# Five rows of a late load go through GpSimd's queue in two blocks of partitions, and two partitions through SyncE

## The chip, the cores and the metric

The kernel runs on one core of a Trainium2 chip. The core has a matrix engine (TensorE, PE in the profile), VectorE (DVE), ScalarE (ACT), GpSimd (POOL) and SyncE (SP), an on-chip memory of 128 partitions, and 16 DMA engines that move data between it and HBM. The metric is the device time of one execution in microseconds (us); smaller is better.

## The reference

The input is an image of 384 x 384 positions with 384 channels in bf16. Each channel's mean over all positions is multiplied by one weight and put through a sigmoid, and every position is multiplied by the 384 scales that result:

```python
H = W = C = 384
def reference(x, w1d):          # x: (1, H, W, C), w1d: (1,)
    g = jnp.einsum("bhwc->bc", x) / (H * W)
    gp = jnp.pad(g, ((0, 0), (0, 0)))
    s = gp[:, 0:C] * w1d[0]
    s = sigmoid(s)
    return x * s[:, None, None, :]
```

Nothing can be written before everything has been read once. The input has 113.2 MB, far more than the on-chip memory, so part of it has to be read a second time.

## The kernel before, in words

A partition gets 1152 of the 147,456 positions, and one position, 384 channels of one partition (768 bytes), is called a row here. One buffer, `arena`, has 275 rows in each partition.

**First pass.** Every row is loaded and summed: `sum_rows` (L253) issues one matmul per row with a matrix of ones, all into one accumulator (L242). 784 rows per partition are only streamed through; 368 rows stay on chip for the second pass. To make room, 296 of these are folded by `fold` (L292): the few exponent bits in which bf16 values of this size differ leave room in three rows for the content of a fourth. VectorE does that with bit operations (lines 276 and 282), ScalarE checks that the values fit (L313). The rows of a fourth are first loaded behind the group's other rows and become free when their group has been folded. For the last group of the second column they are the eight rows `V` (arena rows 212 to 219), so `V` can only be loaded again after the last fold's VectorE steps have read it.

**The end of the first pass** is a list of loads of plain kept rows, each followed by its matmuls, in this order (L443): eight rows at U, 20 at A, 11 at A + 20, eight at A + 31, eight at V, six at Y + 1, four at T + 5, three at T + 2, two at T, and then one last streamed row (L445). T and Y are scratch rows of `fold`. All are issued through SP's queue by `load` (L231, the DMA at L236), 128 partitions each. SP issues in order, and a DMA whose room isn't free yet holds up those behind it.

**The turn.** When the last matmul is done, ScalarE makes the scales `s_bf` (L451) and a copy in the accumulator's bank (L455). GpSimd then scales three blocks of four rows (U, U + 4 and V), and VectorE begins with all other kept rows (`scale`, L464).

**Second pass.** The 784 streamed rows are loaded again, scaled and stored, while the folded groups are unfolded, scaled and stored. The order of loads, stores and scalings is laid down at build time by a small simulation with fixed costs. It begins at the turn and doesn't depend on how the first pass was loaded.

**Order and waits.** The class `Flow` records each step with what it reads and writes (`add`, L34). `emit` (L68) then gives each engine its steps in the order of recording and puts in the semaphore waits. Each DMA is given one of 24 semaphores of its queue in turn, and it waits until the DMA that had this semaphore before has landed. Of a step's waits, the last is attached to its instruction and the others are wait instructions of their own (L112). For a step whose function returns no instruction, the last wait is dropped.

**GpSimd's queue before.** GpSimd issues no DMA in the first pass. Late in the second, the step `again` (L552, recorded at L738) waits for stores, reads a flag, and only if a value didn't fit when folded does it load, scale and store rows anew with GpSimd's own DMAs. For this input the branch isn't taken.

Of the kernel before, what the change touches and what calls it, by code (L numbers as in the profile page):

```python
# [9 lines left out]


class Step:
    __slots__ = ("eng", "emit", "dma", "lane", "deps", "wanted", "rank", "waits", "know", "i")

    def __init__(self, eng, emit, dma):
        self.eng, self.emit, self.dma = eng, emit, dma
        self.deps, self.wanted, self.rank, self.waits, self.know = [], False, 0, [], None
        self.lane = None


class Flow:
# [6 lines left out]
    def __init__(self, nc, tc):  # L28
# [2 lines left out]
        self.writer, self.readers = {}, {}  # L31
        self.queued = {}

    def add(self, eng, emit, reads=(), writes=(), dma=False, after=()):  # L34
        s = Step(eng, emit, dma)
        s.i = len(self.steps)
        deps = set(after)
        for c in reads:
            if c in self.writer:
                deps.add(self.writer[c])  # L40
        for c in writes:
            if c in self.writer:
                deps.add(self.writer[c])
            for r in self.readers.get(c, ()):
                deps.add(r)
        if dma:
            q = self.queued.setdefault(eng, [])
            s.lane = (eng, len(q) % self.LANES)
            s.rank = len(q) // self.LANES + 1
            if len(q) >= self.LANES:  # L50
                deps.add(q[-self.LANES])
            q.append(s)
        for d in deps:
            if d.eng == eng and not d.dma and not dma:

                if eng == "PE":
                    continue
            s.deps.append(d)
        for c in writes:
            self.writer[c] = s  # L60
            self.readers[c] = []
        for c in reads:
            if c not in writes:
                self.readers.setdefault(c, []).append(s)
        self.steps.append(s)
        return s

    def emit(self):  # L68
        nc = self.nc
        engines = {"SP": nc.sync, "ACT": nc.scalar, "PE": nc.tensor, "DVE": nc.vector, "POOL": nc.gpsimd}  # L70

        know = {e: {} for e in engines}

        def covers(k, d):
            return k.get(d.lane, 0) >= d.rank if d.dma else k.get(d.eng, -1) >= d.i

        for s in self.steps:
            k = know[s.eng]
            for d in sorted(s.deps, key=lambda d: -d.i):
                if covers(k, d):  # L80
                    continue
                s.waits.append(d)
                d.wanted = True
                for key, v in d.know.items():
                    if k.get(key, -1) < v:
                        k[key] = v
            s.know = dict(k)
            if s.dma:
                s.know[s.lane] = s.rank
            else:  # L90
                s.know[s.eng] = s.i

        count, sems = {}, {}
        for s in self.steps:
            if not s.dma and s.wanted:
                s.rank = count[s.eng] = count.get(s.eng, 0) + 1

        def sem(s):
            key = s.lane if s.dma else s.eng
            if key not in sems:  # L100
                name = f"f_{key[0]}{key[1]}" if s.dma else f"f_{key}"
                sems[key] = self.tc.alloc_semaphore(name)
            return sems[key]

        last = {}
        with self.tc.tile_critical():  # L106
            for s in self.steps:
                eng = engines[s.eng]
                waits = [(sem(d), d.rank * (16 if d.dma else 1)) for d in s.waits]
                hold = None if s.dma or not waits else waits.pop()  # L110
                for h, v in waits:
                    eng.wait_ge(h, v)  # L112
                ins = s.emit()
                if ins is None:
                    continue
                if hold:
                    ins = ins._wait_ge(*hold)
                if s.dma:
                    ins.then_inc(sem(s), 16)
                    last[s.lane] = s  # L120
                elif s.wanted:
                    ins.then_inc(sem(s), 1)
            for lane, s in sorted(last.items(), key=lambda at: at[1].i):
                engines[lane[0]].wait_ge(sem(s), 16 * s.rank)


# [1 line left out]
def kernel(  # L128
# [11 lines left out]
    nc = tc.nc  # L140
    P = nc.NUM_PARTITIONS
# [13 lines left out]
    PAIR = 2 * PIECE  # L155
    PAIRS = 4
    U = 3 * PIECE + PAIRS * 3 * PAIR
    G0 = U + PAIR
    V = G0 + PAIRS * 3 * PAIR
    A = V + PAIR  # L160
    N_A = 39
    T = A + N_A
    Y = T + 2 * PIECE
# [24 lines left out]
    arena = pool.tile([P, ROWS, C], bf16, name="arena")  # L188
    s_bf = pool.tile([P, C], bf16, name="s_bf")
    rest = pool.tile([P, P], bf16, name="rest")  # L190
    seen = pool.tile([P, 2 * len(pieces)], f32, name="seen")
    odd_i = pool.tile([P, 1], mybir.dt.int32, name="odd_i")
# [6 lines left out]
    xf = x.rearrange("b h w c -> (b h w) c")  # L199
    of = out.rearrange("b h w c -> (b h w) c")  # L200

    def view(t, r0, n):
        return t[r0 * P : (r0 + n) * P, :].rearrange("(p r) c -> p r c", r=n)

    def rows(lo, n):
        return [("a", r) for r in range(lo, lo + n)]

    fl = Flow(nc, tc)
# [5 lines left out]
    STREAMED, KEPT = (0, N_STREAM + 1), (N_STREAM + 1, N_KEPT - 1)  # L214
    LAST_ROW = ROWS - 1
    r = 0
# [7 lines left out]
    def raw(a):  # L224

        return c_raw + 1 + (a - U if a < G0 else PAIR + a - V)
# [4 lines left out]
    def load(chunk, a, lo, hi):  # L231

        r0, n = chunk
        fl.add(
            "SP",
            lambda: nc.sync.dma_start(out=arena[:, a : a + hi - lo, :], in_=view(xf, r0, n)[:, lo:hi, :]),  # L236
            writes=rows(a, hi - lo), dma=True,
        )
    def add_held(rhs, stop=False):

        pe = nc.tensor
        return pe.add_instruction(  # L242
            mybir.InstMatmult(
                name=nc.get_next_instruction_name(),
                ins=[pe.lower_ap(rhs), pe.lower_ap(ones[:])],
                outs=[pe.lower_ap(acc)],
                start_tensor_calc=False, stop_tensor_calc=stop,
                tile_size=(P, P), tile_position=(0, 0), ldweights=False,
            )
        )  # L250


    def sum_rows(a, n):  # L253
        def emit(i, first, last):
            if first:
                return nc.tensor.matmul(acc, lhsT=ones[:], rhs=arena[:, i, :], start=first, stop=last)  # L256
            return add_held(arena[:, i, :], last)

        for i in range(a, a + n):
            first, last = summed[0] == 0, summed[0] == RPP - 1  # L260
            fl.add(
                "PE", lambda i=i, f=first, l=last: emit(i, f, l),
                reads=[("a", i), "ones"], writes=["bank0"],
            )
            summed[0] += 1

    def keep_warm(n):


        for _ in range(n):  # L270
            fl.add("PE", lambda: add_held(s_bf[:]), reads=["s_bf", "ones"], writes=["bank0"])
# [20 lines left out]
    def fold(k):  # L292
# [46 lines left out]
        reads=["ones", "w_bf"], writes=["bank0"],  # L339
# [4 lines left out]
        reads=["bank0"], writes=["w_sc"],  # L344
# [6 lines left out]
    def stream(n, a):  # L351
        load(STREAMED, a, streamed[0], streamed[0] + n)
        if n > 40 and folding:
            keep_warm(N_WARM)
        sum_rows(a, n)
        streamed[0] += n
# [34 lines left out]
    for i, bk in enumerate(banks):  # L391
        lo, hi = i * BANK, min((i + 1) * BANK, PS * C)
# [7 lines left out]
    S1, S2 = [(A, 20)], [(A + 20, N_A - 20)]  # L400
# [38 lines left out]
    def take_raw(a, n):  # L439
        load(KEPT, a, raw(a), raw(a) + n)  # L440
        sum_rows(a, n)

    for a, n in [(U, 8)] + S1 + [(A + 20, 11), (A + 31, 8), (V, 8), (Y + 1, 6), (T + 5, 4), (T + 2, 3), (T, 2)]:  # L443
        take_raw(a, n)
    load(STREAMED, LAST_ROW, N_STREAM, N_STREAM + 1)  # L445
    sum_rows(LAST_ROW, 1)
# [5 lines left out]
        reads=["bank0", "w_sc"], writes=["s_bf"],  # L452
# [96 lines left out]
    N_OVER = 8  # L549
# [23 lines left out]
    written = []  # L573
# [128 lines left out]
    while True:  # L702

        if dve_at <= now:
# [4 lines left out]
            if landed and (ahead < PENDING or not can):  # L709
                chunk, a, lo, n, end = landed.popleft()  # L710
# [13 lines left out]
        if alongside and alongside[0][0] <= now:  # L724
            _, chunk, a, lo, n = alongside.popleft()
            store(chunk, a, lo, lo + n)
            moves.append([now + LAT, n * ROW + PER_STORE, stored(a, n)])
        while waiting and waiting[0][0] <= now:
            _, n, then, chunk, a, lo, known = waiting.popleft()
# [5 lines left out]
            asked = True  # L735
        if out_rows == total and not checked:
            checked = True
            fl.add("POOL", again, reads=["odd_i", "s_bf"], writes=rows(Y, N_OVER), after=written)  # L738
        while over and over[0][0] <= now:
            over.popleft()[1]()  # L740

# [1 line left out]
        if bank_at is None and len(line) <= total - BANKS_AT and got and max(got)[0] > PS * 4 // 3:  # L743
            a = max(got)[1]
# [3 lines left out]
            for i, bk in enumerate(banks):  # L748
                lo, hi = i * BANK, min((i + 1) * BANK, PS * C)
# [6 lines left out]
        if got and todo < N_STREAM:  # L756
            n, a = max(got)
            n = min(n, CAP, N_STREAM - todo)
# [56 lines left out]
```

## Time and profile before

| what | value |
|---|---|
| median of three runs | 720.7 us (720.28 to 720.85) |
| the profiled execution, its own time | 720.22 us |
| its span, first to last instruction | 718.4 us |
| last matmul of the first pass ends, from the span's start | 268.1 us |
| scales ready | 268.7 us |
| read from HBM, written to it | 190.32 MB, 113.25 MB |

The profile shows one execution. Busy time is given by engine; a group of instructions is named by its line, its engine and the buffers written and read. "Idle before" is the time in which the engine stood still before these instructions, with what ended it. The "DMA share" is the mean busy share of the 16 DMA engines and can go a little above 1, since packets overlap. The chain of waits is followed back from the last instruction to what released each step.

### The profile page before, as it was taken

The numbers are of one execution on the slowest core, as the hardware profiler recorded it, in microseconds if no ns is written. First come the engines' busy times: TensorE is split into PE (matmuls) and PEld (weight loads), VectorE is DVE, ScalarE is ACT, GpSimd is POOL, SyncE is SP. The second block draws the span as 40 slices with busy tenths as digits, with TensorE's granted clock in tenths as the row PEclk, the third lists the DMA queues.
The fourth block names the chain that finished last, engine by engine and source line by source line (L and its number), as shares of the span: only waits on it lengthen the run. The fifth ranks groups of instructions, "written<-read, shape, count | busy, mean of one in ns | idle before, by whom it ended". The sixth has DMA issues, their size and how long they took to land.

```text
span 718.4 us, 2070 instructions
## 1 busy us (share of the span) xinstructions
PE 214.4 (30%) x1202; PEld 0.3 (0%) x3; DVE 494.5 (69%) x474; ACT 116.5 (16%) x97; POOL 9.4 (1%) x7
## 2 busy tenths in 40 slices
PE   4667978989887880000000000000000000000000
PEld 0000000000000000000000000000000000000000
DVE  4600001978998929989998999989999965464430
ACT  3700001666777620001000000000000000000000
POOL 0000000000000004000000000000000000000000
PEclk9898999999999995555555555555555555555555
DMA  9999999999999989999999999999999999999997
GB/s 376 440 438 436 438 435 418 434 435 424 423 430 425 427 332 385 402 432 426 423 427 426 431 433 445 420 437 434 435 426 433 431 431 432 432 443 433 424 432 325
DMA packets 19741, 303.69 MB, mean 423 GB/s; under 512 B 2194, under 2 KB 3346, under 8 KB 6290
## 3 DMA queue, kind: packets, MB, share of 16 engines
q1 hardware_dynamic: 19728, 303.57, 99.1%
q8 instruction: 4, 0.07, 0.0%
q14 instruction: 7, 0.06, 0.0%
q10 hardware_dynamic: 2, 0.00, 0.0%
HBM read 190.32 MB, written 113.25 MB: 423 GB/s over the span
## 4 chain that ended last, share of the span: by engine, by line
DMA 72%; DVE 14%; PE 7%; ACT 2%; SPq 0%; issue 0%; another core or an unknown queue 0%; DVEq 0%
DMA arena<-in_x_dram 49%; DMA out_dram<-arena 23%; DVE arena L464 11%; PE bank L242 7%; ACT arena L313 2%; DVE arena L276 2%; DVE arena L282 1%; SPq L236 0%; SPq L474 0%; ACT s_bf L451 0%; SPq L112 0%; DVEq L112 0%; SPq L810 0%; SPq L106 0%
## 5 line engine op out<-in xcount | busy, mean ns | idle before, releaser
L464 DVE TENSOR_TENSOR arena<-arena,s_bf 128x4608 bf16<-128x4608 bf16 (+8 forms) x95 | 228.0, 2431 | 85.6 <-DMA arena<-in_x_dram 71.6
L242 PE MATMUL bank<-arena,ones 128*128 128x384 bf16 x1151 | 206.0, 343 | 44.9 <-DMA arena<-in_x_dram 44.8
L276 DVE TENSOR_SCALAR arena<-arena 128x1536 uint16<-128x1536 uint16 (+2 forms) x247 | 145.1, 632 | 105.5 <-DMA arena<-in_x_dram 99.5
L282 DVE TENSOR_TENSOR arena<-arena 128x1536 uint16<-128x1536 uint16 (+2 forms) x114 | 121.1, 1063 | 10.4 <-PE bank L242 7.6
L313 ACT ACTIVATE arena<-arena 128x3072 uint16<-128x3072 uint16 (+1 forms) x38 | 102.5, 2696 | 143.7 <-DVE arena L276 143.7
L541 PE MATMUL bank<-odd,ones 128*128 128x1 bf16 x1 | 0.2, 186 | 317.4 <-DVE odd L536 317.4
L388 ACT COPY arena<-bank 128x512 uint32<-128x512 uint32 (+2 forms) x8 | 4.2, 533 | 68.9 <-DMA out_dram<-arena 68.7
L464 POOL TENSOR_TENSOR arena<-arena,s_bf 128x1536 bf16<-128x1536 bf16 x3 | 9.2, 3099 | 268.7 <-ACT bank L455 268.7
L464 DVE TENSOR_TENSOR arena<-arena,bank 128x768 bf16<-128x768 bf16 (+5 forms) x12 | 12.5, 1113 | 0.0
L242 PE MATMUL bank<-s_bf,ones 128*128 128x384 bf16 x48 | 8.3, 326 | 0.0
L313 ACT ACTIVATION_READ_ACCUMULATOR arena<-arena 128x1 f32 x38 | 7.1, 186 | 0.0
L388 ACT COPY bank<-arena 128x512 uint32<-128x512 uint32 (+2 forms) x8 | 3.8, 529 | 0.0
L451 ACT ACTIVATE s_bf<-bank,w_sc 128x384 bf16<-128x384 f32 x1 | 0.6, 580 | 12.5 <-PE bank L242 12.5
L256 PE MATMUL bank<-arena,ones 128*128 128x384 bf16 x1 | 0.5, 480 | 6.9 <-DMA arena<-in_x_dram 6.9
L783 ACT ACT_TABLE_LOAD x1 | 1.3, 1283 | 0.7 <-PEq L799 0.7
L333 DVE MEMSET ones<- 128x128 bf16 x1 | 0.2, 165 | 1.1 <-SPq L106 1.1
L338 PE MATMUL bank<-w_bf,ones 1*128 1x1 bf16 x1 | 0.2, 182 | 2.1 <-DMA w_bf<-in_w1d_dram 2.1
L343 DVE TENSOR_SCALAR w_sc<-bank 128x1 f32<-128x1 f32 x1 | 0.2, 159 | 0.9 <-PE bank L338 0.9
L545 DVE CAST odd_i<-bank 128x1 int32<-128x1 f32 x1 | 0.2, 157 | 0.3 <-PE bank L541 0.3
L541 PEld LDWEIGHTS bank<-odd,ones 128*128 128x128 bf16 x1 | 0.1, 104 | 576.3 <-DVE odd L536 576.3
L455 ACT COPY bank<-s_bf 128x192 uint32<-128x192 uint32 x1 | 0.3, 323 | 0.0
L388 ACT COPY arena<-rest 128x64 uint32<-128x64 uint32 x1 | 0.2, 244 | 0.0
(10 smaller groups left out, 1.4 us busy)
## 6 DMA issues: line engine op xcount, KB each, us to landing
arena<-in_x_dram SPq DMA_DIRECT2D x6, 6144.0 KB, 33.8
arena<-in_x_dram SPq DMA_DIRECT2D x6, 4608.0 KB, 28.7
out_dram<-arena SPq DMA_DIRECT2D x8, 3072.0 KB, 30.8
arena<-in_x_dram SPq DMA_DIRECT2D x7, 3072.0 KB, 29.3
out_dram<-arena SPq DMA_DIRECT2D x3, 4608.0 KB, 43.4
arena<-in_x_dram SPq DMA_DIRECT2D x3, 4512.0 KB, 28.8
out_dram<-arena SPq DMA_DIRECT2D x3, 4512.0 KB, 35.4
out_dram<-arena SPq DMA_DIRECT2D x10, 1248.0 KB, 11.1
```

What stands on the lines that cost most here:

```text
L242: return pe.add_instruction(mybir.InstMatmult(name=nc.get_next_instruction_name(), ins=[pe.lower_ap(rhs), pe.lower_ap(ones[:])], outs=[pe. ...
L256: return nc.tensor.matmul(acc, lhsT=ones[:], rhs=arena[:, i, :], start=first, stop=last)
L276: lambda: nc.vector.tensor_scalar(out=dst, in0=src, scalar1=s0, scalar2=s1, op0=op0, op1=op1),
L282: "DVE", lambda: nc.vector.tensor_tensor(out=dst, in0=a, in1=b, op=op), reads=reads, writes=writes
L313: lambda: nc.scalar.activation(out=y, in_=y, func=ACTF.Copy, accum_out=seen[:, 2 * k + i : 2 * k + i + 1]),
L333: fl.add("DVE", lambda: nc.vector.memset(ones[:], 1.0), writes=["ones"])
L388: "ACT", lambda: nc.scalar.copy(dst.bitcast(u32), src.bitcast(u32)), reads=reads, writes=writes
L451: lambda: nc.scalar.activation(out=s_bf[:], in_=acc, func=ACTF.Sigmoid, scale=w_sc[:, 0:1]),
L455: "ACT", lambda: nc.scalar.copy(s_ps.bitcast(u32), s_bf[:].bitcast(u32)), reads=["s_bf"], writes=["bank0"]
L464: lambda: vec.tensor_tensor(out=v, in0=v, in1=s[:, None, :].to_broadcast([P, n, C]), op=Op.mult),
L541: lambda: nc.tensor.matmul(votes, lhsT=ones[:], rhs=odd[:], start=True, stop=True),
L783: nc.scalar.preload_act_table(ACTF.Sigmoid)
```

## The change

The load of eight rows at V is split. Rows V + 5 to V + 7 are loaded as before, through SP with all 128 partitions. Rows V to V + 4 are loaded by three DMAs over different partitions: 121 to 125 (five partitions) and 0 to 120 (121 partitions) through GpSimd's queue, and 126 and 127 through SP. The three are recorded ahead of the load of V + 5, and the matmuls of V + 5 to V + 7 stand ahead of those of V to V + 4.

Since one row now has several writers, `Flow` keeps a list of writers for each row: a step with `part=True` adds itself to the list and doesn't wait for the others in it. All three blocks wait for what read or wrote the rows before. Two smaller edits: the last wait of `again` (`block=True`) is now issued as an instruction of its own instead of being dropped, and the waits at the program's end for the last DMA of each semaphore put GpSimd's queue last.

```diff
+    def add(self, eng, emit, reads=(), writes=(), dma=False, after=(), part=False, block=False):
...
         for c in reads:
-            if c in self.writer:
-                deps.add(self.writer[c])
+            deps.update(self.writer.get(c, ()))
         for c in writes:
-            if c in self.writer:
-                deps.add(self.writer[c])
-            for r in self.readers.get(c, ()):
-                deps.add(r)
+            if not part:
+                deps.update(self.writer.get(c, ()))
+            deps.update(self.readers.get(c, ()))
...
         for c in writes:
-            self.writer[c] = s
+            if part:
+                self.writer[c].append(s)
+                continue
+            self.writer[c] = [s]
             self.readers[c] = []
...
+                if s.block and hold:
+                    eng.wait_ge(*hold)
+                    hold = None
                 ins = s.emit()
...
-            for lane, s in sorted(last.items(), key=lambda at: at[1].i):
+            for lane, s in sorted(last.items(), key=lambda at: (at[0][0] == "POOL", at[1].i)):
                 engines[lane[0]].wait_ge(sem(s), 16 * s.rank)
...
+    FEW, MANY = 5, 11
+    EDGE = MANY * (P // MANY)
+    SHARES = [("POOL", EDGE, EDGE + FEW), ("POOL", 0, EDGE), ("SP", EDGE + FEW, P)]
+
+    def load_upper(chunk, a, lo, hi):
+        r0, n = chunk
+        cells = rows(a, hi - lo)
+        before = {s for c in cells for s in fl.readers.get(c, []) + fl.writer.get(c, [])}
+        for eng, p, q in SHARES:
+            dma = nc.gpsimd if eng == "POOL" else nc.sync
+            fl.add(
+                eng,
+                lambda dma=dma, p=p, q=q: dma.dma_start(
+                    out=arena[p:q, a : a + hi - lo, :], in_=view(xf, r0, n)[p:q, lo:hi, :]
+                ),
+                writes=cells, dma=True, part=p != EDGE, after=before,
+            )
...
-    for a, n in [(U, 8)] + S1 + [(A + 20, 11), (A + 31, 8), (V, 8), (Y + 1, 6), (T + 5, 4), (T + 2, 3), (T, 2)]:
+    N_UPPER = 5
+    for a, n in [(U, 8)] + S1 + [(A + 20, 11), (A + 31, 8)]:
+        take_raw(a, n)
+    load_upper(KEPT, V, raw(V), raw(V) + N_UPPER)
+    take_raw(V + N_UPPER, PAIR - N_UPPER)
+    sum_rows(V, N_UPPER)
+    for a, n in [(Y + 1, 6), (T + 5, 4), (T + 2, 3), (T, 2)]:
         take_raw(a, n)
...
-            fl.add("POOL", again, reads=["odd_i", "s_bf"], writes=rows(Y, N_OVER), after=written)
+            fl.add("POOL", again, reads=["odd_i", "s_bf"], writes=rows(Y, N_OVER), after=written, block=True)
```

More of the change, by code (lines that the diff above doesn't have):

```diff
@@ L12 @@
 class Step:
-    __slots__ = ("eng", "emit", "dma", "lane", "deps", "wanted", "rank", "waits", "know", "i")
+    __slots__ = ("eng", "emit", "dma", "lane", "deps", "wanted", "rank", "waits", "know", "i", "block")
     def __init__(self, eng, emit, dma):
@@ L17, in __init__ @@
         self.deps, self.wanted, self.rank, self.waits, self.know = [], False, 0, [], None
-        self.lane = None
+        self.lane, self.block = None, False
 class Flow:
@@ L32, in __init__ @@
         self.queued = {}
-    def add(self, eng, emit, reads=(), writes=(), dma=False, after=()):
+    def add(self, eng, emit, reads=(), writes=(), dma=False, after=(), part=False, block=False):
         s = Step(eng, emit, dma)
+        s.block = block
         s.i = len(self.steps)
```

## The prediction

> **What bounds the kernel now.** I began with the page's shares, its slices and the chain's summary.
>
> ```profile
> span 718.4 us, 2070 instructions
> DMA  9999999999999989999999999999999999999997
> GB/s 376 440 438 436 438 435 418 434 435 424 423 430 425 427 332 385 402 432 426 423 427 426 431 433 445 420 437 434 435 426 433 431 431 432 432 443 433 424 432 325
> q1 hardware_dynamic: 19728, 303.57, 99.1%
> DMA 72%; DVE 14%; PE 7%; ACT 2%; SPq 0%; issue 0%; another core or an unknown queue 0%; DVEq 0%
> ```
>
> The DMA engines are full all along and 72% of the chain is transfers; one queue, SP's, carries 99.1%. The dip at 332 GB/s is the turn between the passes (slices 15 and 16). The change moves no byte more or less, so it is worth what it does to the turn's time. Next, the chain and the timeline there.
>
> ```profile
> 253.61 0.78 DVE arena L282
> 254.39 9.48 DMA arena<-in_x_dram
> 263.87 0.04 issue
> 263.91 4.23 PE bank L242 x24
> 268.14 0.02 issue
> 268.16 0.59 ACT s_bf L451
> ```
>
> ```profile
> 254.96 0.33 PE L242 MATMUL bank<-arena,ones 128*128 128x384 bf16 x1
> 257.13 6.50 PE L242 MATMUL bank<-arena,ones 128*128 128x384 bf16 x39 [1.84 <-DMA arena<-in_x_dram]
> 263.91 4.21 PE L242 MATMUL bank<-arena,ones 128*128 128x384 bf16 x24 [0.28 <-DMA arena<-in_x_dram]
> ```
>
> The load issued at 254.39 that releases 24 matmuls (8 + 6 + 4 + 3 + 2 + 1) is V, the one that is split. PE hardly rests: the 39 matmuls follow each other every (6.50 - 0.33) / 38 = 0.162 us. From 257.13, when the 20 rows at A have landed, the remaining 63 need at least 62 x 0.162 + 0.33 = 10.4 us, so PE can't end before 267.53. It ends at 263.91 + 4.21 = 268.12. **All that a better order after the load of A can give is 0.59 us.**
>
> The third view is busy time in slices, at the pass's end (columns: stretch, length, engines, PE clock, DMA share, GB/s).
>
> ```profile
> 240.00:254.00 14.00, 11.33 (x60) 0.00 (x0) 12.77 (x19) 9.78 (x7) 0.00 (x0) 0.88 1.01 424
> 255.00:260.00 5.00, 3.16 (x20) 0.00 (x0) 0.55 (x1) 0.65 (x2) 0.00 (x0) 1.00 0.94 347
> 266.00:266.20 0.20, 0.20 (x3) 0.00 (x0) 0.00 (x0) 0.00 (x0) 0.00 (x0) 1.00 0.79 288
> 266.20:266.40 0.20, 0.20 (x3) 0.00 (x0) 0.00 (x0) 0.00 (x0) 0.00 (x0) 1.00 0.77 280
> 266.40:266.60 0.20, 0.20 (x4) 0.00 (x0) 0.00 (x0) 0.00 (x0) 0.00 (x0) 1.00 0.55 200
> 266.60:266.80 0.20, 0.20 (x3) 0.00 (x0) 0.00 (x0) 0.00 (x0) 0.00 (x0) 1.00 0.48 169
> 266.80:267.00 0.20, 0.20 (x3) 0.00 (x0) 0.00 (x0) 0.00 (x0) 0.00 (x0) 1.00 0.34 119
> 267.00:267.20 0.20, 0.20 (x3) 0.00 (x0) 0.00 (x0) 0.00 (x0) 0.00 (x0) 1.00 0.20 65
> 267.20:267.40 0.20, 0.20 (x3) 0.00 (x0) 0.00 (x0) 0.00 (x0) 0.00 (x0) 1.00 0.10 31
> ```
>
> The engines don't finish together. Their idle shares from 266.0 to 267.4 add up to (0.21 + 0.23 + 0.45 + 0.52 + 0.66 + 0.80 + 0.90) x 0.2 = 0.75 us: evenly loaded, they would all end near 266.65 instead of 267.4. One cause is visible. Instruction fetches run on the same engines (first pass; then the stretch 58 to 60 us):
>
> ```profile
> q8 instruction: 4, 0.07, 0.1%
> q14 instruction: 3, 0.02, 0.0%
> ```
>
> ```profile
> q8 instruction: 1, 0.02, 3.0%
> ```
>
> 3.0% of 16 engines over 2 us is 0.96 us on one engine for one fetch. [...]
>
> **The change part by part.**
>
> *The blocks on GpSimd's queue.* Moved are five rows of 126 partitions: at 768 bytes a row 0.48 MB, 1.14 us at the 424 GB/s above (the whole five rows 1.16 us). They leave SP's queue, where V waited 9.48 us behind other loads. GpSimd has nothing else to do here:
>
> ```profile
> 269.17 9.21 POOL L464 TENSOR_TENSOR arena<-arena,s_bf 128x1536 bf16<-128x1536 bf16 x3 [268.73 <-ACT bank L455]
> ```
>
> No DMA issued by GpSimd is in this trace. Lower bound of an issue: SP's 0.44 us (row below); upper: GpSimd's dearest instruction here, 9.21 / 3 = 3.1 us. I take about 1 us each, nearer to the issue than to the arithmetic. Both blocks are then out by about 256.5. In the new order PE wants V to V + 4 behind A + 31 and V + 5: the 21 matmuls that still follow need 20 x 0.162 + 0.33 = 3.6 us, so rows that land by 264.5 leave the end at 268.12. That is 10.1 us after the release at 254.39; at 1.16 us of data this is covered. Without that cover each microsecond past 264.5 is one lost.
>
> *Which engines carry the blocks.* No row tells. Bounds from the tail: at best the blocks fill just what is idle, the last load lands 0.75 us earlier, and PE's 0.59 us caps it. At worst they pile on few engines: 121 partitions x 3840 bytes on one engine, at 424 / 16 = 26.5 GB/s, last 17.5 us and land near 273, some 8 us late. I take the near end, since the tail shows several late engines to relieve. [...]
>
> *What the blocks push back.* Loads issued earlier on SP's queue now share the engines with them.
>
> ```profile
> 252.71 0.33 SPq L236 DMA_DIRECT2D arena<-in_x_dram  x1
> arena<-in_x_dram SPq DMA_DIRECT2D x1, 1056.0 KB, 7.4
> ```
>
> A + 20 (1056 KB, eleven rows) is issued at 252.71 and lands 7.4 us later, 260.1. PE is through with the 20 rows at 257.13 + 20 x 0.162 = 260.4, so there is 0.3 us of room. If all of the blocks' 1.16 us go ahead of it, PE stalls 0.9 us and ends 0.3 us later than before (0.9 - 0.59); if none do, nothing is lost. The blocks come in the middle of this load's transfer: half, 0.58 us late, 0.3 us of stall.
>
> *SP's queue.* One load of V becomes two, one issue more:
>
> ```profile
> 256.74 0.44 SPq L236 DMA_DIRECT2D arena<-in_x_dram  x1
> 255.67 0.33 SPq L236 DMA_DIRECT2D arena<-in_x_dram  x1
> 255.46 0.18 ACT L313 ACTIVATION_READ_ACCUMULATOR arena<-arena 128x1 f32 x1
> ```
>
> From 254.39 two issues of 0.44 end at 255.27, and the next load, Y + 1, waits for ScalarE's check until 255.67 anyway: nothing. Uncovered it would be 0.44 us on loads that land some 10 us after issue. Each later SP DMA gets the next semaphore and so another DMA to wait for, but only for the first 24 of them; these are loads that landed before the turn: nothing.
>
> *PE's waits.* The first matmul of V now waits for three DMAs, two by instructions of their own.
>
> ```profile
> L112 PEldq EVENT_SEMAPHORE  x2: 51/51/51, 1.3 to 9.1; - x2
> L112 POOLq EVENT_SEMAPHORE  x1: 17/17/17, 586.0 to 586.0; - x1
> ```
>
> At most 0.10 us in PE's full stretch, nothing if fetched ahead; 0.05. The restored wait of `again` and the two final waits on GpSimd are such instructions at 0.02 us, beside stores still running: nothing, unless the wait that was dropped came after the last store.
>
> *Sum.* -0.59 (PE's cap) + 0.3 (stall on A + 20) + 0.05 = -0.25 us, against the profiled 720.22: 719.97. The median of the runs is 0.48 above that execution, so 720.45; I say 720.4. Everything after the turn follows the scales and isn't reordered, so it shifts as a whole. 0.2% is 1.44 us, about what a measurement of this kernel can tell from no change, and PE's cap keeps this gain below it.
>
> **The rivals.**
>
> [...]
>
> *Slower: the 121-partition block lands late, 723.2.* If GpSimd takes 3.1 us to issue it and its transfer then lasts as long as V's did (9.48 us), it lands at 254.39 + 3.1 + 9.48 = 267.0; PE ends at 267.0 + 3.6 = 270.6, 2.5 us later. It decides from 264.5 on, and passes 0.2% at 265.9. For it: no row shows what GpSimd's DMA takes; few engines for the block would do the same. Against: an idle queue of its own. [...]
>
> *Faster by more: 719.2.* From 255 to 260 the rate is 347 against 424 GB/s, (1 - 347 / 424) x 5 = 0.9 us lost. If a second queue fills these holes, the load of A lands earlier too, PE's cap moves, and 0.59 + 0.9 = 1.5 us are won. For it: a DMA share of 0.94 there. Against: packets were waiting in SP's queue and still the rate fell.
>
> **How the numbers follow.** The forecast has 0.42, the hidden change 0.21, the late block 0.22, the fuller gain 0.15. The first two are within 0.2%: 0.63 same, 0.22 slower, 0.15 faster. The forecast's own range is 720.1 to 721.0 (cap and full stall). The whole reaches from the faster rival, 719.2, to 723.0, near the slower one's price; half of that rival lies beyond, with the far end where the block piles on one engine.
>
> **What would show it.** Right: the last DMA slices before the turn end more steeply, PE's remaining idle time stands ahead of A + 20 and not ahead of V, the scales come 0 to 0.6 us earlier than 268.74, and the rest is as long as before. Wrong: matmuls that wait for a DMA of GpSimd's after 264.5; a tail as long as before, or longer; a second pass of another length; time between GpSimd's two issues of more than 3 us.

## The result

The changed kernel takes 722.49 us (median of nine runs, 721.54 to 723.97) against 720.28 us (719.53 to 720.85) for the kernel before: 1.0035 times as long, 95% interval 1.0026 to 1.0044. It is slower by 2.2 us by the medians and 2.5 us by the ratio, where 0.3 us less than before was forecast. The profiled execution took 722.83 us, 2.61 more than the one before.

The page of the changed kernel: span, GB/s in 40 slices, the new queue, and the chain's summary.

```profile
span 721.0 us, 2076 instructions
GB/s 383 429 436 434 436 436 414 437 435 428 430 426 427 432 303 335 393 431 424 425 428 426 431 432 442 429 421 441 437 424 441 432 436 432 426 436 434 426 434 341
q0 software_dynamic: 112, 0.48, 0.2%
DMA 68%; DVE 18%; PE 8%; ACT 2%; SPq 0%; issue 0%; another core or an unknown queue 0%; DVEq 0%
```

Slices 15 and 16, the turn, fell from 332 and 385 GB/s to 303 and 335; all others are within 16 GB/s of before. The new queue moved only 0.48 MB. The chain of waits there:

```profile
252.68 10.06 DMA arena<-in_x_dram
262.74 0.04 issue
262.78 8.84 PE bank L265 x43
271.62 0.02 issue
271.65 0.59 ACT s_bf L480
```

The load on the chain is now A + 20, issued at 252.68 and landed at 262.74; before, it was V. The scales are ready at 272.24, 3.49 us later than before. PE's timeline:

```profile
257.10 3.41 PE L265 MATMUL bank<-arena,ones 128*128 128x384 bf16 x20 [1.84 <-DMA arena<-in_x_dram]
262.78 8.83 PE L265 MATMUL bank<-arena,ones 128*128 128x384 bf16 x43 [2.27 <-DMA arena<-in_x_dram]
```

PE is idle for 2.27 us where A + 20 is late. The 43 matmuls after that take 8.83 us, and at 0.162 us each they would take 42 x 0.162 + 0.33 = 7.13: another 1.70 us went. The slices tell why (columns as in the prediction: engines, then PE clock, DMA share, GB/s); the first row is of the kernel before, in the second fence are those of the changed one.

```profile
258.00:263.00 5.00, 5.00 (x33) 0.00 (x0) 0.00 (x0) 0.00 (x0) 0.00 (x0) 1.00 0.99 404
```

```profile
258.00:263.00 5.00, 2.73 (x18) 0.00 (x0) 0.00 (x0) 0.00 (x0) 0.00 (x0) 0.99 1.01 283
263.00:266.00 3.00, 3.00 (x11) 0.00 (x0) 0.00 (x0) 0.00 (x0) 0.00 (x0) 0.50 1.01 408
268.00:269.00 1.00, 1.00 (x8) 0.00 (x0) 0.00 (x0) 0.00 (x0) 0.00 (x0) 1.00 0.11 36
```

From 258 to 263 the 16 engines are as busy as before (1.01), but move 283 GB/s in place of 404: (404 - 283) / 404 x 5 = 1.5 us of transfer lost. The transfers themselves take longer. And after PE's wait its granted clock is 0.50 for three us. The pieces add up: 2.27 (idle) + 1.70 (clock) - 0.59 (what the kernel before lost behind the load of A) = 3.4 us at the turn. Of these 0.9 us come back by the end in this execution.

GpSimd's issues and its block of 121 partitions (454 KB), with the time to landing of A + 20 below:

```profile
253.50 1.23 POOL L256 DMA_DIRECT2D arena<-in_x_dram  x2 [253.06 <-DVE arena L299]
```

```profile
arena<-in_x_dram POOLq DMA_DIRECT2D x1, 453.8 KB, 9.0
arena<-in_x_dram SPq DMA_DIRECT2D x1, 1056.0 KB, 10.1
```

The two issues take 1.23 us together and end at 254.73. The block lands at 263.2; A + 20 needs 10.1 us, 2.7 more than before.

One caution on comparing two profiles here: the stretch 255 to 260 has 347 GB/s in the kernel before and 359 with V split by rows, but 422 in the run with A in two loads and 413 in the one with even and odd partitions, all of which take the same time within the measurement. That dip comes and goes between executions, so verdicts below rest on runs, and traces are used for the rates while the blocks move.

### The profile page after: what moved, and what is told of

It reads as the page before. It is cut to its first block, busy times and chain, and to the rows that moved or that the text cites. A ratio compares the mean times of both kernels' runs of the same rounds, so it can differ in the third digit from the quotient of the medians.

```text
span 721.0 us, 2076 instructions
## 1 busy us (share of the span) xinstructions
PE 215.7 (30%) x1202; PEld 0.3 (0%) x3; DVE 494.6 (69%) x474; ACT 116.5 (16%) x97; POOL 10.6 (1%) x9
## 4 chain that ended last, share of the span: by engine, by line
DMA 68%; DVE 18%; PE 8%; ACT 2%; SPq 0%; issue 0%; another core or an unknown queue 0%; DVEq 0%
DMA arena<-in_x_dram 49%; DMA out_dram<-arena 18%; DVE arena L493 13%; PE bank L265 8%; DVE arena L299 3%; ACT arena L336 2%; DVE arena L305 1%; SPq L241 0%; SPq L503 0%; ACT s_bf L480 0%; SPq L114 0%; DVEq L114 0%; SPq L839 0%; SPq L108 0%
```

## The experiments

Three theories stood at first: the pile-up (the large block puts an uneven share ahead of A + 20), the second queue (GpSimd's transfers slow SP's), and the blocks alone. "Slower" below is against the kernel before.

**The blocks on SP's queue.**

```diff
-    SHARES = [("POOL", EDGE, EDGE + FEW), ("POOL", 0, EDGE), ("SP", EDGE + FEW, P)]
+    SHARES = [("SP", EDGE, EDGE + FEW), ("SP", 0, EDGE), ("SP", EDGE + FEW, P)]
```

> The same three blocks of partitions (121 to 125, 0 to 120, 126 and 127) and the same order of matmuls, but all three issued by SP, in one queue behind A + 20 and A + 31. Theory 1, the pile-up (the 121-partition block puts more than an even share on some engines, ahead of A + 20): here the block can't get ahead of A + 20, so A + 20 lands near 260.1 as before, PE doesn't idle 2.3 us, and only an uneven tail is left: 0 to 1 us slower than before. Theory 2, the second queue (a transfer of GpSimd's beside SP's slows both): with one queue nothing is left, within 0.3 us of before. Theory 3, the blocks alone (121 partitions are a bad shape on any queue): as slow as the change, 2 to 2.5 us slower than before.

Measured 722.24 us, 1.0037 times before (1.0023 to 1.0051). As slow as the change, with GpSimd issuing nothing. A slice while the blocks move, and PE:

```profile
261.00:264.00 3.00, 2.69 (x16) 0.00 (x0) 0.00 (x0) 0.00 (x0) 0.00 (x0) 1.00 1.03 246
```

```profile
257.06 5.20 PE L265 MATMUL bank<-arena,ones 128*128 128x384 bf16 x31 [1.82 <-DMA arena<-in_x_dram]
262.57 1.46 PE L265 MATMUL bank<-arena,ones 128*128 128x384 bf16 x8 [0.31 <-DMA arena<-in_x_dram]
265.79 4.15 PE L265 MATMUL bank<-arena,ones 128*128 128x384 bf16 x24 [1.76 <-DMA arena<-in_x_dram]
```

A + 20 now comes in time (31 matmuls without a break), as all three theories allow, but the rate falls to 246 GB/s all the same, and PE waits 1.76 us for the loads behind the blocks. The loss goes with the blocks, and only its place with the queue. The pile-up theory, which gave 1 us at most, falls too.

**One DMA of 128 partitions on GpSimd's queue.**

```diff
-    SHARES = [("POOL", EDGE, EDGE + FEW), ("POOL", 0, EDGE), ("SP", EDGE + FEW, P)]
+    SHARES = [("POOL", 0, P)]
...
-                writes=cells, dma=True, part=p != EDGE, after=before,
+                writes=cells, dma=True, part=False, after=before,
```

> The five rows of V go through GpSimd's queue in one DMA of 128 partitions, so every DMA engine has its even share; the queue and the early start stay. Theory 1 (pile-up): A + 20 is pushed back by the even share only, 1.16 us at most, to at most 261.3; PE idles under 0.9 us and keeps its clock; 0 to 0.6 us slower than before. Theory 2 (second queue): the rate between 258 and 263 falls as it does in the changed kernel, to some 280 GB/s, and the time is 2 us or more slower than before. Theory 3 (blocks alone): as before, within 0.3 us.

Measured 720.13 us, 1.0011 times before (1.0002 to 1.002).

```profile
258.00:263.00 5.00, 4.72 (x29) 0.00 (x0) 0.00 (x0) 0.00 (x0) 0.00 (x0) 1.00 1.01 416
```

```profile
257.15 3.41 PE L265 MATMUL bank<-arena,ones 128*128 128x384 bf16 x20 [1.84 <-DMA arena<-in_x_dram]
260.84 7.21 PE L265 MATMUL bank<-arena,ones 128*128 128x384 bf16 x43 [0.28 <-DMA arena<-in_x_dram]
```

The second queue costs no rate: 416 GB/s. A + 20 is pushed back by 0.7 us (260.8 in place of 260.1), about what the prediction had for it, and PE idles 0.28 us. The turn is as early as before (the last matmul ends at 268.05), while the runs are 0.3 us slower by the medians and 0.8 by the ratio, 1.4 at most by its interval. So the queue by itself costs little, and not the change's 2.2 to 2.5 us.

**The blocks held back until A + 20 has landed.**

```diff
-                writes=cells, dma=True, part=p != EDGE, after=before,
+                writes=cells, dma=True, part=p != EDGE,
+                after=before | set(fl.writer[("a", A + 20)] if eng == "POOL" else ()),
```

> The changed kernel, but GpSimd's two blocks wait until A + 20 has landed, so they can't push it back; blocks and queue stay. Theory 1 (pile-up ahead of A + 20): A + 20 lands near 260.1, PE idles under 0.4 us there and keeps its clock; the blocks run from about 261 and land near 265, some tenths of a us late for PE; 0 to 1 us slower than before, and 1.5 us or more below the changed kernel. Theory 2 (second queue): the slow stretch only moves to 261 to 266, and the loads in it (A + 31, V + 5, Y + 1) land late instead: 2 us or more slower than before.

Measured 725.5 us, 1.0079 times before (1.0065 to 1.0093): the slowest of all.

```profile
252.69 6.90 DMA arena<-in_x_dram
259.59 0.30 issue
259.89 0.67 POOL arena L256
260.56 7.08 DMA arena<-in_x_dram
267.64 0.10 issue
267.75 5.27 PE bank L266 x21
```

A + 20 lands in time, at 259.6. Now the 121-partition block is the last to land, 7.08 us after its issue, and PE waits 3.65 us for it. The 21 matmuls behind that wait take 5.25 us, and 20 x 0.162 + 0.33 = 3.57 at the full clock: the granted clock is 0.93 from 268 to 269 and 0.50 from 269 to 270, and another 1.7 us went. My expectation of at most 1 us was wrong.

The time to landing alone doesn't show the block as slow, since the DMA of 128 partitions on the same queue also took 7.0 us. The time that GpSimd's packets took does. These are its queue's rows over the stretch 252 to 270 us (packets, MB, share of 16 engines), for the changed kernel, this one and the one with 128 partitions:

```profile
q0 software_dynamic: 112, 0.48, 9.7%
q0 software_dynamic: 112, 0.48, 9.7%
q0 software_dynamic: 80, 0.49, 6.5%
```

The same bytes take half as long again in blocks, ahead of A + 20 or behind it. In the traces' packet records (queue, size, start and time of each packet) one of two partitions (7680 bytes) takes 444 ns on average here, 443 in the changed kernel and 291 with 128 partitions. SP's packets are slowed beside the blocks too: those of 6144 bytes take 361 ns in the changed kernel from 257.9 to 262.3, and 234 beside the 128 partitions (medians). Getting ahead of A + 20 is thus not what makes the blocks dear.

**V split by rows alone.**

```diff
-    SHARES = [("POOL", EDGE, EDGE + FEW), ("POOL", 0, EDGE), ("SP", EDGE + FEW, P)]
+    SHARES = [("SP", 0, P)]
...
-                writes=cells, dma=True, part=p != EDGE, after=before,
+                writes=cells, dma=True, part=False, after=before,
```

> The load of V is split by rows alone: five rows, then three, each with 128 partitions and on SP's queue, with the changed order of matmuls and the two small edits of waits. The theory that the blocks of partitions cost the time: within 0.3 us of before. If the split, the order of the matmuls or the edits of the waits had a part in it: 0.5 us or more slower.

Measured 719.52 us, 0.9994 times before (0.9985 to 1.0003). The split into five and three rows, the order of the matmuls, the added SP issue and the two edits of waits cost nothing that can be told.

**Halves, and even and odd partitions.**

```diff
+        for i, at in enumerate((slice(0, 64), slice(64, P))):          # halves
+        for i, at in enumerate((slice(0, P, 2), slice(1, P, 2))):      # even and odd
...
+                "SP",
+                lambda at=at: nc.sync.dma_start(
+                    out=arena[at, a : a + hi - lo, :], in_=view(xf, r0, n)[at, lo:hi, :]
```

> The five rows go through SP's queue as two blocks, partitions 0 to 63 and 64 to 127. If every one of 16 engines takes an equal share of a 64-partition load, no engine has more to move than before. [...] Theory B (the blocks send several engines to the same part of the on-chip memory): each block reaches one half of the partitions, the rate falls to about half of 420 GB/s while the two blocks move, 0.49 MB take 2.3 us in place of 1.16, and the turn comes some 1 us later; 0.7 to 1.5 us slower than before. [...]

> As the kernel with the two halves, but the blocks are the even and the odd partitions: as many DMAs, bytes and descriptors, and each block reaches over the whole memory. Theory B (same part of the memory): no fall of the rate to half, within 0.5 us of before, and faster than the halves by 0.5 us or more. A theory by which two DMAs of 64 partitions are in themselves dearer than one of 128: the same as the halves.

The halves: 722.0 us, 1.0038 times before (1.0026 to 1.005). Even and odd: 720.0 us, 1.0003 (0.9994 to 1.0012). The same slice of the two kernels, the halves first:

```profile
261.00:264.00 3.00, 2.48 (x16) 0.00 (x0) 0.00 (x0) 0.00 (x0) 0.00 (x0) 1.00 1.03 231
```

```profile
261.00:264.00 3.00, 3.00 (x20) 0.00 (x0) 0.00 (x0) 0.00 (x0) 0.00 (x0) 1.00 1.03 417
```

Two DMAs of 64 partitions each, the same bytes, the same queue: 231 against 417 GB/s at the same busy share. In the packet records a packet of one partition (3840 bytes) takes 254 ns in the halves and 149 in the even and odd blocks (medians). Which partitions go together in a DMA decides. The halves cost more than I expected (1.5 us at most), as much as the change itself.

**112 and 16 partitions, 120 and 8.**

```diff
+        for i, at in enumerate((slice(0, 112), slice(112, P))):        # seven
+        for i, at in enumerate((slice(0, 120), slice(120, P))):        # fifteen
```

> The five rows go through SP's queue as blocks of 112 and 16 partitions. If the engines share a load evenly whenever they can, each of 16 gets seven partitions of the one and one of the other: eight, as before, but the seven don't start where an even load's eight do. If the changed kernel's cost comes from which partitions an engine writes, and not from its uneven shares: the rate falls below 350 GB/s for two us or more and the time is 1 to 2.5 us slower than before. If uneven shares make it: within 0.4 us of before.

> The five rows go through SP's queue as blocks of 120 and 8 partitions. [...] If a fall of the rate comes with any split that doesn't leave each engine its usual partitions: 1 us or more slower.

The first: 721.58 us, 1.0026 times before (1.0015 to 1.0037). The second: 722.27 us, 1.0034 (1.0021 to 1.0046). The same slice, 112 and 16 first:

```profile
261.00:264.00 3.00, 2.60 (x16) 0.00 (x0) 0.00 (x0) 0.00 (x0) 0.00 (x0) 1.00 1.03 238
```

```profile
261.00:264.00 3.00, 1.92 (x13) 0.00 (x0) 0.00 (x0) 0.00 (x0) 0.00 (x0) 1.00 1.02 228
```

Both fall to the rate of the 121-partition block on the same queue (246 GB/s). If 112 and 16 partitions are dealt evenly over 16 engines, which no trace shows, no engine had more to move there than in an even load, and uneven shares aren't needed for the loss. The 120 partitions reach nearly the whole memory and still have 228 GB/s, so how much of it a block reaches doesn't decide alone either. What the runs leave is this: in the slices above the rate is 228 to 283 GB/s with every division into neighbouring ranges that was tried (121 + 5 + 2, 120 + 8, 112 + 16, 64 + 64), and neither with 128 partitions (416) nor with even and odd ones (417) did the rate fall. Each division also changes which addresses of HBM a DMA reads; no run separates that side from the on-chip one.

**GpSimd's blocks in the other order.**

```diff
+    SHARES = [("POOL", 0, EDGE), ("POOL", EDGE, EDGE + FEW), ("SP", EDGE + FEW, P)]
```

> The changed kernel with GpSimd's two blocks in the other order, the 121 partitions first and then the five. [...] Theory B (the 121-partition block is slow wherever it goes): the rate still falls to 250 to 300 GB/s for about five us, A + 20 lands 1 us or more late, and the time is 1.5 to 3 us slower than before.

Measured 723.12 us, 1.0045 times before (1.0031 to 1.0058). A slice while the blocks move:

```profile
259.00:262.00 3.00, 1.91 (x13) 0.00 (x0) 0.00 (x0) 0.00 (x0) 0.00 (x0) 1.00 1.03 269
```

No gain, and the rate falls as before. Which engine a packet ran on the trace doesn't tell.

**Two rows in place of five.**

```diff
-    N_UPPER = 5
+    N_UPPER = 2
```

> The changed kernel with two rows of V in the blocks in place of five, the other six through SP with 128 partitions. If the cost goes with the bytes that move in blocks of partitions (theory B): two fifths of the changed kernel's 2.2 to 2.6 us, 0.7 to 1.2 us slower than before. If it is a cost per DMA of GpSimd's or per block, whatever the size: 2 us or more slower than before.

Measured 720.68 us, 1.0015 times before (1.0006 to 1.0024), about 0.9 to 1.1 us (0.4 to 1.7 by the interval). That is near two fifths of the change's cost for two fifths of the bytes, and less than the 2 us that a price per DMA would give. But the size isn't all that differs, as GpSimd's issues and the slice 249 to 253 show:

```profile
245.55 1.23 POOL L256 DMA_DIRECT2D arena<-in_x_dram  x2 [245.10 <-DVE arena L299]
249.00:253.00 4.00, 1.88 (x10) 0.00 (x0) 3.77 (x7) 2.91 (x3) 0.00 (x0) 0.92 1.03 377
```

The first two rows of V are free earlier, so GpSimd issues the blocks 8 us earlier than in the changed kernel. They move ahead of the load of A, at 377 GB/s from 249 to 253 (424 in the kernel before), and the load of A lands at 258.1 in place of 257.1. PE then runs through without a wait and ends at 268.50, 0.4 us later than before. So a smaller price for fewer bytes is shown, and not that the price is proportional to them.

This trace also tells how GpSimd's 121 partitions were cut into packets. Its packet records have 30 packets of three partitions, 15 of two and one of one, which fits fifteen equal shares of eight partitions (3 + 3 + 2) and a share of one. The changed kernel's 60 packets of two partitions and one of one fit the same shares. Whether a share went to one engine the records don't tell.

**PE's clock.** The changed kernel with work for PE during the wait, twice, and the changed kernel again, unaltered.

```diff
     for a, n in [(U, 8)] + S1 + [(A + 20, 11), (A + 31, 8)]:
+        if a == A + 20:
+            keep_warm(14)
         take_raw(a, n)
```

> The changed kernel with 14 more matmuls on zeros between the 20 rows at A and the 11 at A + 20, 14 x 0.162 = 2.3 us of PE work in the place where PE stands idle for 2.27 us. Theory 1 with the clock: the matmuls after the idle stretch run at half the granted clock for ten rows, which costs 10 x 0.16 = 1.6 us; with PE kept busy they don't, and the time is 1.2 to 1.8 us below the changed kernel's, about 0.7 to 1 us slower than before. If only the late landing of A + 20 counts and the clock is a side effect that the wait for data would hide, the time is that of the changed kernel.

> The changed kernel once more, unaltered, beside the three others. By its first runs: 2 to 2.6 us slower than before. In its profile A + 20 lands 1 us or more later than 260.1 and the rate from 258 to 263 is near 280 GB/s; whether PE's clock halves again after the wait is open.

> The changed kernel with 14 matmuls on zeros ahead of A + 20, a second time and now beside the changed kernel on one chip. If the halved clock costs what one profile shows, 1.6 us, it is 1.2 to 1.8 us below the changed kernel. If the clock drops only in some executions, as the first runs suggest, it is 0 to 0.7 us below.

Kept busy: 722.05 us, 1.003 times before (1.0019 to 1.004), and 722.07, 1.003 (1.0019 to 1.0042). The changed kernel again: 723.06, 1.0047 (1.0034 to 1.0061). In that last profile the clock did not drop at the turn:

```profile
257.02 3.41 PE L265 MATMUL bank<-arena,ones 128*128 128x384 bf16 x20 [1.84 <-DMA arena<-in_x_dram]
262.09 1.95 PE L265 MATMUL bank<-arena,ones 128*128 128x384 bf16 x11 [1.66 <-DMA arena<-in_x_dram]
264.68 5.36 PE L265 MATMUL bank<-arena,ones 128*128 128x384 bf16 x32 [0.65 <-DMA arena<-in_x_dram]
```

After 1.66 us of idle time the 11 matmuls take 1.95 us, as 10 x 0.162 + 0.33 = 1.95 says for the full clock; the turn was 1.6 us earlier than in the first profile of the same kernel. So the halved clock comes in some executions and not in all. The length of the wait alone doesn't decide: in the kernel before and in the changed one PE waits 2.61 us for data that land near 243.6, and from 245 to 247 its clock is 0.50 in the first and 1.00 in the second. Keeping PE busy brought the two medians down by 0.4 and 1.0 us, with overlapping intervals. With it the kernel is still some 2.2 us slower than before, so the greater part of the loss is the late data; how much the clock adds on average isn't settled.

**A in two loads of ten rows, on the kernel before.**

```diff
-    for a, n in [(U, 8)] + S1 + [(A + 20, 11), (A + 31, 8), (V, 8), (Y + 1, 6), (T + 5, 4), (T + 2, 3), (T, 2)]:
+    for a, n in [(U, 8), (A, 10), (A + 10, 10), (A + 20, 11), (A + 31, 8), (V, 8), (Y + 1, 6), (T + 5, 4), (T + 2, 3), (T, 2)]:
```

> The kernel before, with the load of 20 rows at A in two of ten rows each, so that PE, idle from 255.3 until all 20 have landed at 257.1, can begin some 2.3 us earlier. If PE's lack of room (0.59 us) sets the turn: up to 0.5 us faster than before. If the last loads' landing sets it: within 0.3 us, not to be told from before.

Measured 719.8 us, 0.9999 times before (0.999 to 1.0008). PE starts earlier and then waits more often:

```profile
254.98 1.79 PE L242 MATMUL bank<-arena,ones 128*128 128x384 bf16 x10
257.03 1.78 PE L242 MATMUL bank<-arena,ones 128*128 128x384 bf16 x10 [0.26 <-DMA arena<-in_x_dram]
259.58 3.30 PE L242 MATMUL bank<-arena,ones 128*128 128x384 bf16 x19 [0.77 <-DMA arena<-in_x_dram]
263.27 4.20 PE L242 MATMUL bank<-arena,ones 128*128 128x384 bf16 x24 [0.38 <-DMA arena<-in_x_dram]
```

PE ends at 267.47 here, 0.65 us earlier than in the profile before, but in a stretch without the dip (422 GB/s from 255 to 260); the runs show no gain, as the second expectation said. No version that was run is shown to be faster than the kernel before.

## Why the prediction was wrong

- **What bounds the kernel: right.** What was lost came from the turn, and the second pass followed it, but for the 0.9 of 3.5 us that came back by the end.
- **The blocks on GpSimd's queue: right in the price of the issue and in the cover, wrong in the transfer.** An issue takes 0.6 us (1 us was taken). The block lands at 263.2, ahead of the 264.5 from which it would cost PE. But its packets take half as long again as those of a 128-partition load (9.7 against 6.5% of the engines), and that the 1.16 us of data didn't allow for.
- **Which engines carry the blocks: the step that failed.** I weighed engines with more or fewer partitions, at a rate of 26.5 GB/s for each, and took the near end. The rate was the thing that moved: 283 GB/s over 16 engines in place of 404. The halves (231 GB/s) and the 112 + 16 blocks (238) have the same fall, and no run shows that some engines had more to move there. That the blocks load or relieve single engines was my estimate throughout, as was the even share in a load of 128 partitions: the trace doesn't tell which engine a packet ran on. The packets of the 121 partitions fit fifteen equal shares of eight and one of one.
- **What the blocks push back: right mechanism, wrong size.** I gave A + 20 0.3 us of stall, 0.9 at most. It was 2.27 us in one profile and 1.66 in the other, since the transfers that shared the stretch became slower. At the full rate, with 128 partitions on the same queue, it was 0.28 us, as forecast.
- **SP's queue and the waits: right.** With V split by rows alone these edits are all there, and the time is 0.9994 times before.
- **PE's cap: right, but with no reserve on the other side.** After the wait of 2.27 us the clock was also down to 0.50 in one profile, 1.70 us that had no term in the sum.
- **The rivals.** "Slower" had 0.22 and a price of 723.2 by another mechanism: the block late for PE behind its own queue. That the measured 722.49 came near this price is luck. In the changed kernel PE waited for A + 20 and not for the block; only when the blocks were held back did the block itself come last. The "hidden change", which has 0.21 among the chances, stood for a change that gains nothing at the turn. V split by rows (0.9994) and the 128 partitions on GpSimd's queue (1.0011) are such changes, this one isn't: 1.0035 times before. So a second queue by itself gained nothing, and no run shows a price for uneven shares of the engines.
- **The tail.** The uneven end of the first pass that the change could have used is real in the trace, but the last slice above (36 GB/s from 268 to 269) shows it later than before, when it ended near 267.4. That instruction fetches make it uneven, as the prediction has it, no run tests; three of the seven fetches moved only 0.02 MB together.
- **The sum.** Its three terms give -0.24 and not -0.25 us, which doesn't matter.

## What to carry to other kernels

A load with fewer partitions than 128 may not be just a share of a full one: check its rate (here 228 to 283 GB/s in the blocks, 416 with all 128), not only its bytes and its engines. Before dividing a transfer to even out the DMA engines, compare what can be won (here 0.75 us of idle time, 0.59 of it usable) with the whole stretch running at 55 to 70% of its rate (231 of 417 and 283 of 404 GB/s). And when an experiment undoes one property at a time (queue, order, size, partitions), the one with the same bytes and a different layout tells most.

## What the hardware did that I had not expected

The DMA engines stay at a busy share of 1.0 while they move 228 to 283 GB/s, so the busy share alone shows nothing of this loss; the GB/s beside it does. Ranges of neighbouring partitions did it in every split of the five rows that was tried, even and odd partitions didn't (417 GB/s). Why packets take longer beside the blocks (SP's of 6144 bytes 361 ns, against 234 beside the 128 partitions) isn't settled, nor whether on the on-chip side or in HBM: the trace doesn't tell which engine a packet ran on. And PE's granted clock fell to 0.50 for three us after 2.27 us of idle time in one execution, and not after 1.66 us in another; after 2.61 us it was 0.50 in one execution and 1.00 in another. What decides it no run shows.
